# Reading the moving tiles of f32r products by 64-byte pieces, in six different orders

## The chip, the cores and the metric

The kernel runs on one core of a Trainium2 chip. The metric is device time in microseconds for one execution, from the first to the last instruction of the program with what lies around it, as the median of several executions. A profile is one further execution, recorded instruction by instruction. The core has a matrix engine (TensorE, PE in the profile, with its weight loads shown apart as PEld), VectorE (DVE), ScalarE (ACT), GpSimd (POOL), and SyncE (SP), which issues the DMAs.

## The reference

Eight batches of eight heads, 576 tokens, 64 values a head. In each head 32 packed queries p attend over k and v; then the tokens' queries q attend over the 32 packed results, which serve as keys and values. The heads' outputs, side by side, are a row of 512 per token, and all 4608 rows go through a gated feed-forward block with 1536 inner columns.

```python
def sm_attn(qq, kk, vv):
    s = scale * np.matmul(qq, kk.transpose(0, 1, 3, 2))
    s = s - np.max(s, axis=-1, keepdims=True)
    a = np.exp(s)
    a = a / (np.sum(a, axis=-1, keepdims=True) + 1e-09)
    return np.matmul(a, vv)
p_packed = sm_attn(p, k, v)
out = sm_attn(q, p_packed, p_packed)
...
g = x @ w_gate
silu = g * (1.0 / (1.0 + np.exp(-g)))
val = x @ w_val
return (silu * val @ w_out).astype(np.float32)
```

The weights w_gate, w_val and w_out arrive as 64-bit floats, the rest as 32-bit floats.

## The kernel before

A batch's second attention never forms its output. Its weights a2 (one column per token, 32 rows for each head, so two tiles of 128 rows by 576 tokens) are multiplied by a matrix that has the packed values already multiplied into w_gate and w_val. That matrix is built for each batch and each pair of inner chunks by `m_mm` (L586, with `by_head`, L267).

The inner dimension is cut into 12 chunks (`fc`) of 128. `gv_chunk` (L619) makes a chunk of gate and a chunk of value for the first or second part of a batch's tokens: 256 and 320 tokens (`NA`, `NB`); odd batches take the 320 first. The moving operand of these products (L633) is a2, with 256 or 320 columns, one per token; the stationary one is the folded matrix. The result, in PSUM, has the inner columns as rows and the tokens as columns. ScalarE takes the SiLU of the gate (L640), VectorE multiplies by the value (L644), and the product becomes the stationary operand of the second multiplication. There `out_mm` (L650, matmuls at L652) takes 128 tokens at a time, with 512 columns of w_out as the moving operand, and adds up over the 12 chunks in an accumulator `acc`. w_out lies in six tiles, one per pair of chunks; `w_[fc // 2][:, fc % 2]` is one chunk of 512 columns.

Both products are done in f32r, a 32-bit type with a shorter mantissa. Each operand is rounded to it (the high part), and what the rounding left is kept as a second f32r tile (the low part); a product is the sum of high x high, high x low and low x high, three matmuls (`mh`/`ml`, `a2h`/`a2l`, `hh`/`hl`, `wo_h`/`wo_l`). In batch 0 the first ten chunks' output products and the first four chunks' gate and value products are plain f32 instead (L828, L787), and its gate and value products are written apart, in `gv` (L774).

Each batch has 64 tokens that fill no whole row tile; those of two batches are kept in `t4`, and after every odd batch their 128 rows are multiplied by w_out in one go, 36 matmuls without a break between them except for other work put in the middle (`mm4`, the tiles named `aux` at L652).

What sets the order: on TensorE the program order by hand, `PROGRAM` for batch 0 and the tables `FIRST` and `LATER` for the attention steps of later batches, which are put in between the pieces of `gv_chunk` and `outs`. The other engines work beside it and are waited for by semaphores. All this is untouched by the change; it touches the matmuls at L633, L652 and L828 and, on the host, the layout of `q` and `w_out`, before either goes to the chip.

Of the kernel before, what the change touches and what calls it, by code (L numbers as in the profile page):

```python
# [20 lines left out]
B, H, S, D = 8, 8, 576, 64  # L21
NP = 32
DM, DF = 512, 1536
P = 128
NPAR, NHP = 2, 4
NFC = DF // P
# [6 lines left out]
NA, NB = 256, 320  # L33
# [3 lines left out]
F64_HI_MOST = float(np.array(0x47EFFFFF, np.int32).view(np.float32))  # L37
SPLIT = 5
PAD = 120
LOW_WORD = -(2.0**-51) * 15 / 16  # L40

PROGRAM = """

# [89 lines left out]
def tile_pack_attention_swiglu(ctx: ExitStack, tc: tile.TileContext, qT, kT, v, vq, pT, wgv, wout, out):  # L133
# [57 lines left out]
    def f64_convert(dst, st, shape):  # L191
# [5 lines left out]
        yield nc.scalar.activation(dst, hi.bitcast(F32), AF.Abs)  # L197
        yield nc.scalar.activation(lo.bitcast(F32), lo.bitcast(U32), AF.Identity, bias=minus_two, scale=LOW_WORD)
        yield nc.vector.tensor_scalar(dst, dst, F64_HI_LEAST, F64_HI_MOST, op0=ALU.max, op1=ALU.min)
# [3 lines left out]
    sts, wos, wo_h, wo_l = {}, {}, {}, {}  # L203
# [58 lines left out]
    def by_head(outs, lhs, rhs):  # L262

        for hp in range(NHP):
            for par in range(NPAR):
                r = slice(64 * par, 64 * par + 64)
                nc.tensor.matmul(outs[par][32 * hp : 32 * hp + 32], lhs(r, hp), rhs(r, hp), start=True, stop=True)  # L267
# [90 lines left out]
    def s1_scale(b):  # L358
        pp = pool.tile([P, NPAR * D + PAD], F32, tag="pp", bufs=1, name="pp")[:, : NPAR * D].rearrange(
            "p (r d) -> p r d", r=NPAR  # L360
        )
        nc.vector.tensor_tensor(
            pp,
            pps[b][0][:, : NPAR * D].rearrange("p (r d) -> p r d", r=NPAR),
            st1[b][2][:, 2].unsqueeze(2).broadcast_to([P, NPAR, D]),
            op=ALU.mult,
        )
        pps[b].append(pp)
# [241 lines left out]
    def h_split(src, hi, lo, between=lambda: False, tag=""):  # L610
        hh, hl = (pool.tile([P, 256], F32R, tag=t + tag, bufs=2, name=t) if tag else h_tile(t) for t in ("hh", "hl"))
        copy(hi, hh, src)
        last = between()
        low = lo.tensor_tensor(hl, src, hh.bitcast(F32), op=ALU.subtract)  # L614
        if last:
            pin(low)
        return hh, hl

    def gv_chunk(b, fc, is_b, fill, behind, between):  # L619
        odd = b % 2  # L620
        n = NB if is_b else NA
        off = (0 if odd else 256) if is_b else (320 if odd else 0)
        mh, ml = ms[b, fc // 2]
        ah, al = a2[b]
        f = fc % 2
        pgs = []
        for s in range(2):
            pg = ps_gv.tile([P, 512], F32, tag="gv", name="gv")
            pgs.append(pg)
            i = 0  # L630
            for m_, a_ in ((ml, ah), (mh, al), (mh, ah)):
                for g in range(NPAR):
                    nc.tensor.matmul(  # L633
                        pg[:, :n], m_[:, g, f, s * P : (s + 1) * P], a_[:, g, off : off + n],
                        start=(i == 0), stop=(i == 5),
                    )
                    i += 1
            fill()
        sg = pool.tile([P, NB], F32, tag="sg", bufs=1, name="sg")
        nc.scalar.activation(sg[:, :n], pgs[0][:, :n], AF.Silu)  # L640
        behind()
        hf = pool.tile([P, 256], F32, tag="hf", bufs=2, name="hf")
        o, o4 = (64, 0) if is_b and odd else (0, 256)
        nc.vector.tensor_tensor(hf, pgs[1][:, o : o + 256], sg[:, o : o + 256], op=ALU.mult)  # L644
        if is_b:
            r, r4 = slice(64 * odd, 64 * odd + 64), slice(o4, o4 + 64)
            nc.vector.tensor_tensor(t4[b // 2][:, fc, r], pgs[1][:, r4], sg[:, r4], op=ALU.mult)
        return h_split(hf, nc.scalar, nc.vector, between)

    def out_mm(acc, hh, hl, c, fc):  # L650
        for i, (h_, w_) in enumerate(((hl, wo_h), (hh, wo_l), (hh, wo_h))):
            nc.tensor.matmul(  # L652
                acc[:, :],
                h_[:, c : c + P],
                w_[fc // 2][:, fc % 2],
                start=(fc == 0 and i == 0),
                stop=(fc == NFC - 1 and i == 2),
            )
# [60 lines left out]
    with tc.manual_schedule(engines={mybir.EngineType.PE}):  # L719
# [19 lines left out]
        with tc.manual_schedule(  # L739
# [18 lines left out]
            rows, accs = [], []  # L758
# [33 lines left out]
            def half(i):  # L792
                fc, is_b = order[i]
                if fc // 2 < SPLIT:
                    return h0[fc // 2][:, fc % 2, 256 * is_b : 256 * is_b + 256]
                if i not in hs:
                    hs[i] = [pool.tile([P, 256], F32, tag="hf", bufs=2, name="hf")]
                return hs[i][0]
# [23 lines left out]
            def outs(i):  # L822
                fc, is_b = order[i]
                for c in range(2):
                    if fc // 2 >= SPLIT:
                        out_mm(accs[2 * is_b + c], *hs[i][1:], c * P, fc)
                        continue
                    nc.tensor.matmul(  # L828
                        accs[2 * is_b + c], half(i)[:, c * P : c * P + P], wos[fc // 2][:, fc % 2],
                        start=(fc == 0), stop=(fc == NFC - 1),  # L830
                    )

# [23 lines left out]
            def half_of(f, b):  # L856
# [5 lines left out]

            words = {
                "g": gv, "silu": silu, "h": hmul, "hh": h_high, "hl": h_low, "out": outs,
                "z_scores": lambda x: (None if x else s1_tile(0), s1_scores(0, x)), "z_max": lambda x: s1_max(0, x),
                "z_top": lambda x: s1_top(0), "z_exp": lambda x: s1_exp(0, True), "z_turn": lambda x: s1_turn(0, x),
# [26 lines left out]
        def last_outs(rows, accs, out):  # L893
# [5 lines left out]
            return last  # L899

        behind = last_outs(rows, accs, lambda which: outs(2 * NFC - 2 + which))

        steady[0] = True
        def batch(b, behind):
# [6 lines left out]
            def outs(fc, which, fill=lambda: None):  # L911
                src = (hb if which else ha).pop(fc)
                for c in range(2):
                    out_mm(accs[2 * which + c], *src, c * P, fc)
                    fill()

            for fc in range(NFC):
                count = [0]

                def fill():  # L920
                    count[0] += 1
                    if count[0] == 2:
                        run(fc, 2)
                        if fc == NFC - 1 and b + 1 < B:
                            m_part(b + 1, 0, both)
                        elif fc % 2 and fc + 1 < NFC:
                            m_part(b, (fc + 1) // 2, both)
                    if b == 1 and 1 <= fc <= 2 * SPLIT - 4 and count[0] == 7:
                        wout_high(fc + 3)
                        wout_low(fc + 3)  # L930
                    if count[0] != 2:
                        run(fc, count[0])

                ha[fc] = gv_chunk(b, fc, False, fill, lambda: run(fc, "a"), lambda: run(fc, "ha"))
                m_lows()
                if fc:
                    outs(fc - 1, 0, fill)
                else:
                    behind(0)
                hb[fc] = gv_chunk(b, fc, True, fill, lambda: run(fc, "b"), lambda: run(fc, "hb"))  # L940
                if fc:
                    outs(fc - 1, 1, fill)
                else:
                    behind(1)
                    for x, y in zip((rows, accs), accs_of(b)):
                        x.extend(y)
# [11 lines left out]
            def mm4(*ks):  # L958
                for k in ks:
                    for i in range(2):  # L960
                        out_mm(p4[0], *halves[k], i * P, 2 * k + i)
# [59 lines left out]
```

## Time and profile before

| what | value |
|---|---|
| time, median of 3 runs | 735.1 us (735.01 to 736.07) |
| the profiled execution's own time | 734.87 us |
| its span, first to last instruction | 733.1 us |
| TensorE busy | 723.9 us (99%) |
| VectorE busy | 454.2 us (62%) |
| ScalarE busy | 373.7 us (51%) |
| read from HBM, written | 48.69 MB, 9.49 MB |
| share of 16 DMA engines on the main queue | 21.9% |

A busy share of 99% on TensorE doesn't say that it runs at its best, since matmuls overlap and each row holds the time in which the result drains: two matmuls that start 0.23 us apart can each show 0.39 us. To see what a matmul costs in a stream, one takes the distance of two starts. "Idle before" is the time for which an engine did nothing ahead of the instructions of a group, with what ended it. In names such as `acc<-wo_h,hl` the result stands on the left, then the moving and the stationary operand.

### The profile page before, as it was taken

The page shows a single profiled execution, that of the slowest core. Times are in us where ns is not written, and L with a number is a line of the kernel's source. Part 1 is how long each engine was busy: PE and PEld are TensorE (multiplying, and loading weights), DVE is VectorE, ACT ScalarE, POOL GpSimd, SP SyncE. Part 2 cuts the span into 40 slices and gives each one's busy share as a digit, 9 for nine tenths or more (in the row PEclk, how much of TensorE's full clock was granted, in tenths as well). Part 3 has the DMA queues.
Part 4 walks back from the last instruction along what each step waited for, and adds up shares of the span by engine and source line. Part 5 has one row for each costly group of instructions (what it writes and reads, how often), then busy time and mean ns, then how long its engine had stood idle before and what let it go on. Part 6 is the DMA issues. An engine that isn't in the chain of part 4 may idle for free.

```text
span 733.1 us, 15099 instructions
## 1 busy us (share of the span) xinstructions
PE 723.9 (99%) x6242; PEld 590.4 (81%) x6242; DVE 454.2 (62%) x1009; ACT 373.7 (51%) x668; POOL 2.0 (0%) x13
## 2 busy tenths in 40 slices
PE   8899999999999999999999999999999999999997
PEld 4655667888888888888888888888888888888886
DVE  4999779665755557664764646665574655744333
ACT  3779737754635445553563535654453535533331
POOL 0000000000000000000000000000000000000000
PEclk9999999999999999999999999999999999999999
DMA  9697482310112201302112011102001000010001
GB/s 344 269 346 276 140 315 95 111 73 2 65 58 85 74 1 66 126 4 73 66 48 93 21 57 65 43 19 73 1 2 72 4 2 1 1 59 1 1 1 72
DMA packets 20004, 59.15 MB, mean 81 GB/s; under 512 B 5984, under 2 KB 7008, under 8 KB 17376
## 3 DMA queue, kind: packets, MB, share of 16 engines
q1 hardware_dynamic: 19792, 58.12, 21.9%
q8 instruction: 49, 0.80, 0.5%
q14 instruction: 19, 0.16, 0.1%
q10 hardware_dynamic: 144, 0.07, 0.0%
HBM read 48.69 MB, written 9.49 MB: 79 GB/s over the span
## 4 chain that ended last, share of the span: by engine, by line
PE 96%; DVE 1%; issue 0%; DVEq 0%
PE gv L633 36%; PE acc L652 34%; PE aux L267 7%; PE gv L787 6%; PE acc L828 5%; PE aux L652 4%; PE gv_aux L482 1%; PE gv_aux L398 1%; PE gv_aux L267 1%; DVE w L200 0%; PE acc L726 0%; PE aux L343 0%; DVE w L201 0%; PE aux L324 0%; DVE ot L180 0%; PE aux L398 0%
## 5 line engine op out<-in xcount | busy, mean ns | idle before, releaser
L640 ACT ACTIVATE sg<-gv 128x256 f32<-128x256 f32 (+1 forms) x168 | 69.0, 411 | 175.3 <-PE gv L633 161.6
L644 DVE TENSOR_TENSOR hf<-gv,sg 128x256 f32<-128x256 f32 x168 | 71.0, 422 | 129.8 <-PE gv L633 118.5
L633 PE MATMUL gv<-a2h,ml 128*128 128x256 f32 (+1 forms) x672 | 143.5, 295 | 0.0
L633 PE MATMUL gv<-a2l,mh 128*128 128x256 f32 (+1 forms) x672 | 143.4, 295 | 0.0
L633 PE MATMUL gv<-a2h,mh 128*128 128x256 f32 (+1 forms) x672 | 143.4, 295 | 0.0
L652 PE MATMUL acc<-wo_h,hl 128*128 128x512 f32 x344 | 139.8, 406 | 0.0
L652 PE MATMUL acc<-wo_l,hh 128*128 128x512 f32 x344 | 135.5, 394 | 0.0
L652 PE MATMUL acc<-wo_h,hh 128*128 128x512 f32 x344 | 135.5, 394 | 0.0
L633 PEld LDWEIGHTS gv<-a2h,ml 128*128 128x128 f32 x672 | 116.4, 189 | 15.3 <-ACT sg L803 0.4
L178 ACT CAST hh<-hf 128x256 fp32r<-128x256 f32 x168 | 67.7, 403 | 101.9 <-DVE hf L644 101.8
L633 PEld LDWEIGHTS gv<-a2l,mh 128*128 128x128 f32 x672 | 107.8, 189 | 0.0
L633 PEld LDWEIGHTS gv<-a2h,mh 128*128 128x128 f32 x672 | 107.6, 188 | 0.0
L614 DVE TENSOR_TENSOR hl<-hf,hh 128x256 fp32r<-128x256 f32 x168 | 69.8, 416 | 46.4 <-ACT hh L178 46.3
L652 PEld LDWEIGHTS acc<-wo_h,hl 128*128 128x128 f32 x344 | 64.5, 188 | 28.0 <-issue 19.2
L652 PEld LDWEIGHTS acc<-wo_h,hh 128*128 128x128 f32 x344 | 64.6, 188 | 14.6
L652 PEld LDWEIGHTS acc<-wo_l,hh 128*128 128x128 f32 x344 | 64.6, 188 | 8.3 <-issue 0.2
L571 DVE TENSOR_TENSOR ml<-aux,mh 128x512 fp32r<-128x512 f32 x92 | 58.9, 682 | 5.4 <-ACT mh L597 5.4
L267 PE MATMUL aux<-w,ppt 64*32 64x512 f32 (+1 forms) x784 | 52.1, 588 | 0.9 <-DVE w L201 0.9
L597 ACT CAST mh<-aux 128x512 fp32r<-128x512 f32 x92 | 49.4, 590 | 5.6 <-PE aux L267 1.2
L640 ACT ACT_TABLE_LOAD x30 | 38.5, 1283 | 13.6 <-PE gv L633 9.8
L828 PE MATMUL acc<-wo_f,h 128*128 128x512 f32 x80 | 37.8, 602 | 0.0
L828 PEld LDWEIGHTS acc<-wo_f,h 128*128 128x128 f32 x80 | 14.2, 189 | 16.7 <-issue 16.2
(153 smaller groups left out, 754.3 us busy)
## 6 DMA issues: line engine op xcount, KB each, us to landing
st<-in_wgv SPq DMA_DIRECT2D x12, 1024.0 KB, 7.6
k_t<-in_kT SPq DMA_DIRECT2D x16, 576.0 KB, 4.9
q_t<-in_qT SPq DMA_DIRECT2D x16, 576.0 KB, 4.9
out<-ot SPq DMA_DIRECT2D x36, 256.0 KB, 2.1
v_t<-in_vq SPq DMA_DIRECT2D x6, 1280.0 KB, 5.7
st<-in_wout SPq DMA_DIRECT2D x6, 1024.0 KB, 6.8
v_t<-in_v SPq DMA_DIRECT2D x2, 1024.0 KB, 8.7
p_t<-in_pT SPq DMA_DIRECT2D x7, 64.0 KB, 2.4
```

The costliest lines, as they stand in the source:

```text
L178: e.copy(dst, src)
L267: nc.tensor.matmul(outs[par][32 * hp : 32 * hp + 32], lhs(r, hp), rhs(r, hp), start=True, stop=True)
L398: nc.tensor.matmul(pss[par][NP * j : NP * j + NP, i * SQ : (i + 1) * SQ], p_t[r, 2 * g + i, :], k_t[r, j // 2, 2 * g + i, j % 2 * SQ : j % ...
L571: pin(nc.vector.tensor_tensor(*lows.pop(0), op=ALU.subtract))
L597: nc.scalar.copy(m[0][at], src)
L614: low = lo.tensor_tensor(hl, src, hh.bitcast(F32), op=ALU.subtract)
L633: nc.tensor.matmul(pg[:, :n], m_[:, g, f, s * P : (s + 1) * P], a_[:, g, off : off + n], start=(i == 0), stop=(i == 5),)
L640: nc.scalar.activation(sg[:, :n], pgs[0][:, :n], AF.Silu)
L644: nc.vector.tensor_tensor(hf, pgs[1][:, o : o + 256], sg[:, o : o + 256], op=ALU.mult)
L652: nc.tensor.matmul(acc[:, :], h_[:, c : c + P], w_[fc // 2][:, fc % 2], start=(fc == 0 and i == 0), stop=(fc == NFC - 1 and i == 2),)
L787: nc.tensor.matmul(held[i][s][:, :n], m_[:, g, f, s * P : (s + 1) * P], a_[:, g, off : off + n], start=(j == 0), stop=(j == len(todo) - 1),)
L828: nc.tensor.matmul(accs[2 * is_b + c], half(i)[:, c * P : c * P + P], wos[fc // 2][:, fc % 2], start=(fc == 0), stop=(fc == NFC - 1),)
```

## The change

A moving operand that was read from its first column to its last is read in pieces of 16 columns (64 bytes in each partition), and the order of the pieces is one of six. A pair (folds, sign) names an order: the pieces are dealt into `folds` equal runs; the reader takes the first piece of each run, then the second of each, and so on, and with sign -1 it goes through the runs from their last pieces to their first. Within a piece the columns ascend. `UP`, (1, 1), is the order of before and keeps the plain pattern.

- `GV_WALK`, by batch: batches 0, 1 and 7 as before, 2 descending, 3 two runs backward, 4 two runs forward, 5 four runs forward, 6 four runs backward.
- `OUT_WALK`, by pair of w_out's chunks: pair 0 as before, then descending, two runs backward, two runs forward, four runs forward, four runs backward.

The columns of q (hence of a2, which is made from it column by column) and those of w_out are laid out in HBM so that the walk meets them in their natural order: the results land in PSUM as before, in one run, and all that follows is the same. 256 columns make 16 pieces, 320 make 20, 512 make 32.

Nothing moves: each engine issues the same instructions in the same order, with the same waits, and the same DMAs.

```diff
+LINE = 16
+UP, DOWN = (1, 1), (1, -1)
+GV_WALK = (UP, UP, DOWN, (2, -1), (2, 1), (4, 1), (4, -1), UP)
+OUT_WALK = (UP, DOWN, (2, -1), (2, 1), (4, 1), (4, -1))
...
+def walk(n, way):
+    folds, sign = way
+    lines = n // LINE // folds
+    return (0 if sign > 0 else LINE * (lines - 1)), [(sign * LINE, lines), (LINE * lines, folds), (1, LINE)]
+
+
+def places(n, way):
+    start, ((s0, n0), (s1, n1), (s2, n2)) = walk(n, way)
+    i, j, k = np.ogrid[:n0, :n1, :n2]
+    return (start + s0 * i + s1 * j + s2 * k).ravel()
...
-                        pg[:, :n], m_[:, g, f, s * P : (s + 1) * P], a_[:, g, off : off + n],
+                        pg[:, :n], m_[:, g, f, s * P : (s + 1) * P], walked(a_[:, g, off : off + n], GV_WALK[b]),
...
+    def walked(x, way):
+        if way == UP:
+            return x
+        (p0, pn), (step, n) = x.ap
+        start, dims = walk(n, way)
+        return bass.AP(x.tensor, x.offset + start, [(p0, pn), *((k, m) for k, m in dims if m > 1)])
+
     def out_mm(acc, hh, hl, c, fc):
         for i, (h_, w_) in enumerate(((hl, wo_h), (hh, wo_l), (hh, wo_h))):
             nc.tensor.matmul(
                 acc[:, :],
                 h_[:, c : c + P],
-                w_[fc // 2][:, fc % 2],
+                walked(w_[fc // 2][:, fc % 2], OUT_WALK[fc // 2]),
...
                     nc.tensor.matmul(
-                        accs[2 * is_b + c], half(i)[:, c * P : c * P + P], wos[fc // 2][:, fc % 2],
+                        accs[2 * is_b + c], half(i)[:, c * P : c * P + P],
+                        walked(wos[fc // 2][:, fc % 2], OUT_WALK[fc // 2]),
...
-    qT, kT = heads_t(q), heads_t(k)
+    q_laid = np.empty_like(q)
+    for b in range(B):
+        at = 0
+        for n in (NB, NA) if b % 2 else (NA, NB):
+            q_laid[b][:, at + places(n, GV_WALK[b])] = q[b][:, at : at + n]
+            at += n
+    qT, kT = heads_t(q_laid), heads_t(k)
...
-    wo = np.ascontiguousarray(wo).reshape(NFC, P, DM).view(np.int64)
+    wo_laid = np.empty(wo.shape, wo.dtype).reshape(NFC, P, DM)
+    for fc in range(NFC):
+        wo_laid[fc][:, places(DM, OUT_WALK[fc // 2])] = wo[fc * P : (fc + 1) * P]
+    wo = wo_laid.view(np.int64)
```

## The prediction

> **What bounds the kernel now.** I read the head of the page first, then the chain that ended last, then the groups with shapes kept apart, and last the timeline of TensorE in two stretches. The head and the chain:
>
> ```profile
> span 733.1 us, 15099 instructions
> PE 723.9 (99%) x6242; PEld 590.4 (81%) x6242; DVE 454.2 (62%) x1009; ACT 373.7 (51%) x668; POOL 2.0 (0%) x13
> ...
> PEclk9999999999999999999999999999999999999999
> ...
> PE 96%; DVE 1%; issue 0%; DVEq 0%
> PE gv L633 36%; PE acc L652 34%; PE aux L267 7%; PE gv L787 6%; PE acc L828 5%; PE aux L652 4%; PE gv_aux L482 1%; PE gv_aux L398 1%; PE gv_aux L267 1%; DVE w L200 0%; PE acc L726 0%; PE aux L343 0%; DVE w L201 0%; PE aux L324 0%; DVE ot L180 0%; PE aux L398 0%
> ```
>
> TensorE is the chain: 96% of the span by engine, at a granted clock that never leaves the top digit. L633 and L652 are 36 + 34 + 4 = 74% of it, and L828 another 5%: exactly the matmuls whose moving operand the change reads differently. So no engine stands between the change and the end: what one such matmul gains or loses is gained or lost in full. The spacing of the starts is what counts, since a matmul's own row also holds the time in which its result drains. Two stretches of the timeline of TensorE (columns: start in us, duration, engine, line, operation, tiles, shape, count):
>
> ```profile
> 139.38 0.45 PE L633 MATMUL gv<-a2h,ml 128*128 128x320 f32 x2
> ...
> 140.84 0.45 PE L633 MATMUL gv<-a2h,mh 128*128 128x320 f32 x2
> 141.13 0.39 PE L652 MATMUL acc<-wo_h,hl 128*128 128x512 f32 x1
> ...
> 142.52 0.40 PE L633 MATMUL gv<-a2h,ml 128*128 128x256 f32 x2
> ...
> 143.70 0.40 PE L633 MATMUL gv<-a2h,mh 128*128 128x256 f32 x2
> ...
> 209.42 0.39 PE L652 MATMUL aux<-wo_h,hl 128*128 128x512 f32 x1
> ...
> 214.66 0.39 PE L652 MATMUL aux<-wo_h,hh 128*128 128x512 f32 x1
> 214.88 0.45 PE L633 MATMUL gv<-a2h,ml 128*128 128x320 f32 x2
> ```
>
> Ten matmuls of 320 columns start between 139.38 and 140.84, so 146 ns each; ten of 256 between 142.52 and 143.70, 118 ns each; six of 512 between 141.13 and 142.52, 232 ns each. One column more costs (232 - 118) / 256 = 0.44 ns. In the long stretch that begins at 209.42 twenty-four matmuls of 512 columns fit into 5.46 us, 227 ns each, with the same operands.
>
> **The change part by part.** Every engine issues the same instructions in the same order with the same waits, and no DMA changes its size or its shape: the columns of q and of w_out lie in another order in HBM, and the copies, the splits and the softmax work on them column by column as they lie. These parts cost nothing, and no cover is needed for that. What is left is the read pattern of TensorE's moving operand. How many are affected follows from the rows of the groups, shapes kept apart:
>
> ```profile
> L652 PE MATMUL acc<-wo_h,hl 128*128 128x512 f32 x344 | 139.8, 406 | 0.0
> ...
> L633 PE MATMUL gv<-a2h,ml 128*128 128x320 f32 x336 | 76.5, 309 | 0.0
> ...
> L633 PE MATMUL gv<-a2h,mh 128*128 128x256 f32 x336 | 67.1, 281 | 0.0
> ...
> L828 PE MATMUL acc<-wo_f,h 128*128 128x512 f32 x80 | 37.8, 602 | 0.0
> ...
> L652 PE MATMUL aux<-wo_l,hh 128*128 128x512 f32 x48 | 18.7, 390 | 0.0
> ```
>
> Output products: 344 + 48 = 392 in each of the three terms. Those with pair 0 of w_out stay as they are: seven batches x two chunks x four row tiles = 56 in acc and 8 in aux. So 328 a term, 984 in all, are read in 32 pieces, with 31 jumps between them: 30,504 jumps. Gate and value products: 3 terms x 672 = 2016 over batches 1 to 7; batches 2 to 6 are walked, 1440 of them, half with 16 pieces and half with 20: 720 x 15 + 720 x 19 = 24,480 jumps. L828 (batch 0, plain f32): 64 of its 80 rows, 1984 jumps. Together about **57,000 jumps**. With 0.2% of the time, 1.5 us, as about what a measurement of this kernel can tell from no change, the whole question is whether one jump costs more than 1.5 us / 57,000 = **0.026 ns**, a sixteenth of a column.
>
> No row of before shows TensorE reading a moving operand in pieces. The nearest rows are those of the other engines that read SBUF in pieces, or with a step:
>
> ```profile
> L530 ACT ACTIVATE s<-s 128x576 f32<-128x576 f32 x16 | 11.0, 686 | 5.0 <-DVE s L526 4.9
> ...
> L420 ACT ACTIVATE e<-e 128x576 f32<-128x576 f32 x12 | 8.2, 687 | 0.1
> ...
> L178 ACT CAST hh<-hf 128x256 fp32r<-128x256 f32 x168 | 67.7, 403 | 101.9 <-DVE hf L644 101.8
> ...
> L197 ACT ACTIVATE wo_f<-st 128x1024 f32<-128x1024 f32 x6 | 6.9, 1154 | 2.3 <-DMA st<-in_wout 2.3
> ...
> L229 ACT CAST wo_h<-wo_f 128x512 fp32r<-128x512 f32 x12 | 7.4, 613 | 1.5 <-DVE wo_f L201 1.5
> ```
>
> L420 and L530 are the same exponential over 576 elements; L530 reads one run, L420 four runs of 144 words: 687 against 686 ns, so three jumps cost nothing to see. L197 takes every second word, a jump at every element. ScalarE's adjacent reads cost (613 - 403) / 256 = 0.82 ns an element, so 1024 of them would take 613 + 512 x 0.82 = 1033 ns; L197 took 1154, 0.12 ns a jump (its function is another one, so this is an upper end). VectorE shows the same step:
>
> ```profile
> L614 DVE TENSOR_TENSOR hl<-hf,hh 128x256 fp32r<-128x256 f32 x168 | 69.8, 416 | 46.4 <-ACT hh L178 46.3
> ...
> L201 DVE SCALAR_TENSOR_TENSOR wo_f<-st,wo_f 128x1024 int32<-128x1024 int32 x6 | 7.3, 1220 | 0.1
> ...
> L233 DVE TENSOR_TENSOR wo_l<-wo_f,wo_h 128x512 fp32r<-128x512 f32 x12 | 8.2, 683 | 0.4
> ```
>
> Adjacent: 1.04 ns an element ((683 - 416) / 256), so 1024 would take 683 + 534 = 1217 ns; L201, with one operand read every second word, took 1220. Nothing again.
>
> The bounds of a jump are then 0 (L420, L201), 0.12 ns (L197, + 57,000 x 0.12 = 6.8 us) and, since TensorE takes a column in about half the time that ScalarE takes for an element, and a reader that stops for a column at each jump is the plainest way to lose time, 0.44 ns (57,000 x 0.44 = +25 us). Below nothing the bound is the spare time in the spacing of 512-column matmuls, 232 against 227 ns: 3 x (344 - 56) = 864 walked ones in acc x 5 ns = -4.3 us. I take **0 per jump**: L420 is the row nearest in kind, runs of adjacent 4-byte words with jumps between.
>
> [...]
>
> Could the longer pattern cost time per instruction rather than per jump? This row from the timeline bounds it:
>
> ```profile
> 417.61 0.59 PE L482 MATMUL gv_aux<-v_t,a 128*32 128x32 f32 x16
> ```
>
> Sixteen small matmuls, each with its own weights, take 0.59 us, 37 ns apiece with the drain. So an instruction is taken in within 37 ns, beside the 118 ns of the shortest walked matmul; some 80 ns of cover remain. If that cover were gone, each ns would cost 2424 walked f32r matmuls x 1 ns = 2.4 us.
>
> The sum: 734.87 us (the profiled execution: span 733.1 and 1.8 around it) + 0 = 734.9. That execution lies 0.2 us under the median, so the forecast is **735.1 us**.
>
> **The rivals.** *Slower: TensorE's reader loses time at a jump.* Place: L633 in batches 2 to 6 and L652 at pairs 1 to 5. Price: at 0.12 ns a jump 741.9 us, at a column 760. It decides from 0.026 ns a jump. For it: TensorE takes a column in 0.44 ns where ScalarE takes 0.82, so a hiccup that those engines' rows hide may show here; a reader that fetches ahead in ascending order may miss at the backward steps. And every f32r matmul has little slack. Against it: L420 and L201. A milder form, where only backward or folded orders pay, falls between. Chance 0.23, half of it below 745.
>
> *Faster: the order takes off some of the spacing.* The 232 ns of acc against 227 in the long stretch is a loss that some order might avoid: 735.1 - 4.3 = 730.8 us. Against it: the long stretch reads the same wo_h and wo_l by the same ascending order and has the 227, so the loss goes with what was issued just before, not with how the columns are read. [...] Chance 0.06.
>
> *No effect: only the sequence of addresses differs.* That is the forecast, 735.1, with the chance that is left: 0.71.
>
> **How the numbers follow.** The likeliest case is no change, 735.1, give or take the 1 us between runs. The range leaves out the slower half of the slower rival (0.11) and most of the faster one: 733.4 to 745.0; it takes in the 0.12 ns bound. Faster by over 0.2% 0.06, within 0.2% 0.71, slower by over 0.2% 0.23.
>
> **What would show it.** The spare-row products (L652 into aux) run 24 + 12 in a row after each pair of batches, six with each pair of w_out, hence six with each of the six orders, the old one first: if a jump costs nothing, all keep 227 ns; if it costs a column, the first six keep 227 and the others take 227 + 31 x 0.44 = 241. Batches 2 to 6 must keep the 118 and 146 ns of batches 1 and 7. If the starts keep their spacing and the time still moved, the cause is outside TensorE's reading and the argument above is wrong; if only some orders pay, the rule of one price for every jump is wrong.

## The result and the profile after

The changed kernel takes 741.4 us (741.35 to 741.63 in four runs) against 735.1 us: a ratio of 1.0085, 95% interval 1.0068 to 1.0102, so slower by 6.4 us. I had given no change the best chance; the time lies inside the range.

The page of the profiled execution (741.35 us, of which the span is this), head and chain:

```profile
span 739.6 us, 15099 instructions
PE 730.8 (99%) x6242; PEld 593.6 (80%) x6242; DVE 454.6 (61%) x1009; ACT 374.0 (51%) x668; POOL 2.0 (0%) x13
...
PEclk9999999999999999999999999999999999999999
...
PE 96%; DVE 1%; issue 0%; DVEq 0%
PE gv L651 36%; PE acc L677 34%; PE aux L285 7%; PE gv L812 5%; PE acc L853 5%; PE aux L677 5%; PE gv_aux L500 1%; PE gv_aux L416 1%; PE gv_aux L285 1%; DVE w L218 0%; PE acc L751 0%; PE aux L361 0%; DVE w L219 0%; PE aux L342 0%; DVE ot L198 0%; PE aux L416 0%
```

The lines have moved: L633 is now L651, L652 is L677, L828 is L853. TensorE is busy 6.9 us more, VectorE and ScalarE 0.4 and 0.3 us, and the chain is the same. L853, the plain f32 products of which 64 of 80 rows are walked, kept 37.8 us and a mean of 602 ns. The place that tells the orders apart is the long stretch of spare-row products after batch 1, where the six orders follow one another, six matmuls each. Its timeline, with the first start of each order:

```profile
209.67 0.39 PE L677 MATMUL aux<-wo_h,hl 128*128 128x512 f32 x1
...
211.05 0.40 PE L677 MATMUL aux<-wo_h,hl 128*128 128x512 f32 x1
...
212.46 0.40 PE L677 MATMUL aux<-wo_h,hl 128*128 128x512 f32 x1
...
213.86 0.40 PE L677 MATMUL aux<-wo_h,hl 128*128 128x512 f32 x1
...
215.30 0.46 PE L651 MATMUL gv<-a2h,ml 128*128 128x320 f32 x2
...
217.06 0.39 PE L677 MATMUL aux<-wo_h,hl 128*128 128x512 f32 x1
...
218.47 0.39 PE L677 MATMUL aux<-wo_h,hl 128*128 128x512 f32 x1
...
219.89 0.40 PE L651 MATMUL gv<-a2h,ml 128*128 128x256 f32 x2
```

A sixth of each distance is the price of one matmul: contiguous 1.38 / 6 = 230 ns, descending 235, two runs backward 233, two runs forward 240, four runs forward 235, four runs backward 237. The orders differ, although each of the five new ones has 31 jumps. Averaged over all starts of the trace (distances that hold other work left out), before and after:

| order | 512 columns in acc, before | after | 512 in aux, after | batch: 256 columns | 320 columns |
|---|---|---|---|---|---|
| contiguous | 231.5 | 231.0 | 230.8 | 1: 117.8 | 146.2 |
| descending | 231.5 | 233.6 | 233.6 | 2: 118.1 | 147.2 |
| two runs backward | 231.4 | 232.9 | 233.8 | 3: 119.0 | 148.8 |
| two runs forward | 231.6 | 239.9 | 239.6 | 4: 120.1 | 151.5 |
| four runs forward | 231.6 | 234.3 | 233.9 | 5: 118.8 | 147.0 |
| four runs backward | 230.9 | 237.2 | 238.0 | 6: 119.0 | 146.2 |

(ns from start to start; before, the two right columns are 117.9 and 146.1 in every batch, within 0.2, and aux has 226.7 to 230.3.) Going backward is not what costs: the dearest order, two runs forward, steps through both runs in ascending order. Where the time went: acc has 168 matmuls for each pair, 192 for the last: 168 x (-0.5 + 2.1 + 1.5 + 8.3 + 2.7) + 192 x 6.3 ns = 3.6 us; aux, 24 each, 1.0 us; a2's products, 144 of each size in each batch, 2.2 us. That is 6.8 us, against 6.5 in the spans.

### The profile page after: what moved, and what is told of

The parts are those of the page before. It is cut to its first block, busy times and chain, and to the rows that moved or that the text cites. A ratio compares the mean times of both kernels' runs of the same rounds, so it can differ in the third digit from the quotient of the medians.

```text
span 739.6 us, 15099 instructions
## 1 busy us (share of the span) xinstructions
PE 730.8 (99%) x6242; PEld 593.6 (80%) x6242; DVE 454.6 (61%) x1009; ACT 374.0 (51%) x668; POOL 2.0 (0%) x13
## 4 chain that ended last, share of the span: by engine, by line
PE 96%; DVE 1%; issue 0%; DVEq 0%
PE gv L651 36%; PE acc L677 34%; PE aux L285 7%; PE gv L812 5%; PE acc L853 5%; PE aux L677 5%; PE gv_aux L500 1%; PE gv_aux L416 1%; PE gv_aux L285 1%; DVE w L218 0%; PE acc L751 0%; PE aux L361 0%; DVE w L219 0%; PE aux L342 0%; DVE ot L198 0%; PE aux L416 0%
## 5 line engine op out<-in xcount | busy, mean ns | idle before, releaser
L651 PE MATMUL gv<-a2h,ml 128*128 128x256 f32 (+1 forms) x672 | 144.3, 296 | 0.0
L651 PE MATMUL gv<-a2l,mh 128*128 128x256 f32 (+1 forms) x672 | 144.2, 296 | 0.0
L651 PE MATMUL gv<-a2h,mh 128*128 128x256 f32 (+1 forms) x672 | 144.1, 296 | 0.0
L677 PE MATMUL acc<-wo_h,hl 128*128 128x512 f32 x344 | 141.5, 411 | 0.0
L677 PE MATMUL acc<-wo_l,hh 128*128 128x512 f32 x344 | 136.8, 398 | 0.0
L677 PE MATMUL acc<-wo_h,hh 128*128 128x512 f32 x344 | 136.6, 397 | 0.0
L651 PEld LDWEIGHTS gv<-a2h,ml 128*128 128x128 f32 x672 | 116.8, 188 | 16.3 <-ACT sg L828 0.4
L651 PEld LDWEIGHTS gv<-a2h,mh 128*128 128x128 f32 x672 | 108.1, 188 | 0.0
L651 PEld LDWEIGHTS gv<-a2l,mh 128*128 128x128 f32 x672 | 108.0, 188 | 0.0
L677 PEld LDWEIGHTS acc<-wo_h,hl 128*128 128x128 f32 x344 | 64.7, 188 | 28.2 <-issue 19.2
L677 PEld LDWEIGHTS acc<-wo_h,hh 128*128 128x128 f32 x344 | 64.8, 188 | 16.0
L677 PEld LDWEIGHTS acc<-wo_l,hh 128*128 128x128 f32 x344 | 64.8, 188 | 8.5 <-issue 0.2
L853 PE MATMUL acc<-wo_f,h 128*128 128x512 f32 x80 | 37.8, 602 | 0.0
L853 PEld LDWEIGHTS acc<-wo_f,h 128*128 128x128 f32 x80 | 14.2, 189 | 16.7 <-issue 16.2
```

What stands on the lines that cost most here:

```text
L651: nc.tensor.matmul(pg[:, :n], m_[:, g, f, s * P : (s + 1) * P], walked(a_[:, g, off : off + n], GV_WALK[b]), start=(i == 0), stop=(i == 5),)
L677: nc.tensor.matmul(acc[:, :], h_[:, c : c + P], walked(w_[fc // 2][:, fc % 2], OUT_WALK[fc // 2]), start=(fc == 0 and i == 0), stop=(fc == ...
L853: nc.tensor.matmul(accs[2 * is_b + c], half(i)[:, c * P : c * P + P], walked(wos[fc // 2][:, fc % 2], OUT_WALK[fc // 2]), start=(fc == 0), ...
```

## The experiments

The rival prices were now: one price per jump (0.11 ns would make the 6.4 us), a collision of the moving reads with the next matmul's weight load, or a loss of the reader's own that depends on the order. Four of the runs put stretches of equal matmuls behind the kernel before; each of them is one execution, with a granted clock of 1.0, and a price in them is the distance from a stretch's first start to the next stretch's, divided by 40. The contiguous order of 512 columns, with 128 stationary columns that start on a multiple of 256 bytes, took 226.7 to 228.2 ns in its stretches, so a difference of about 1.5 ns between two stretches says nothing.

**Orders, widths and columns.** Added to the kernel before, behind its last instruction: stretches of 40 f32r matmuls into one PSUM tile, here those with 512 columns and 128, 64 or 32 stationary columns.

```diff
+        def read(x, at, *dims):
+            return bass.AP(x.tensor, x.offset + at, [x.ap[0], *dims])
+        mv, wt = wo_l[0][:, 0], wo_h[5]
+        N = 40
+        pt = ps()
+        for i in range(N):
+            nc.tensor.matmul(pt[:128, :512], wt[:, 0, 0:128], read(mv, 0, (16, 16), (256, 2), (1, 16)), start=(i == 0), stop=(i == N - 1))
...
```

> The kernel before, with 20 stretches of 40 f32r matmuls added at its end, each stretch one order of reading, one width of the stationary operand and one number of columns. Two theories. Reader theory: the moving operand's reader alone loses time, by the order: with 512 columns about 227 ns a matmul for ascending, 233 descending, 233 two runs backward, 240 two runs forward, 234 to 237 for four runs, at 128, 64 and 32 stationary columns alike; and the loss grows with the columns: two runs forward 120 ns at 256, 150 at 320, 180 at 384, ascending 113, 142, 170. Collision theory: the next matmul's weight load and the moving reads get in each other's way, and the order decides how often: with 64 stationary columns half of the loss over 213 ns goes (ascending 220, two runs forward 227), with 32 three quarters (217, 220); and the loss per matmul is about the same at 256 as at 512 columns. One price per jump, whatever the order: 234 ns for all five new orders at 512 columns.

The timeline of the stretches (start, length of the 40 together). L992 is contiguous, L995 descending, L998 two runs backward, L1001 two runs forward, L1004 four runs forward; L1019 and L1031 are two runs forward with 64 and 32 stationary columns:

```profile
728.65 9.23 PE L992 MATMUL aux<-wo_l,wo_h 128*128 128x512 f32 x40
737.72 9.50 PE L995 MATMUL aux<-wo_l,wo_h 128*128 128x512 f32 x40
747.05 9.50 PE L998 MATMUL aux<-wo_l,wo_h 128*128 128x512 f32 x40
756.39 9.76 PE L1001 MATMUL aux<-wo_l,wo_h 128*128 128x512 f32 x40
765.99 9.49 PE L1004 MATMUL aux<-wo_l,wo_h 128*128 128x512 f32 x40
775.32 9.70 PE L1007 MATMUL aux<-wo_l,wo_h 128*128 128x512 f32 x40
...
812.60 9.76 PE L1019 MATMUL aux<-wo_l,wo_h 128*64 128x512 f32 x40
822.20 9.36 PE L1022 MATMUL aux<-wo_l,wo_h 128*64 128x512 f32 x40
...
850.06 9.76 PE L1031 MATMUL aux<-wo_l,wo_h 128*32 128x512 f32 x40
859.66 6.03 PE L1034 MATMUL aux<-wo_l,wo_h 128*128 128x320 f32 x40
865.52 6.29 PE L1037 MATMUL aux<-wo_l,wo_h 128*128 128x320 f32 x40
871.65 4.95 PE L1040 MATMUL aux<-wo_l,wo_h 128*128 128x256 f32 x40
876.44 4.96 PE L1043 MATMUL aux<-wo_l,wo_h 128*128 128x256 f32 x40
881.24 7.12 PE L1046 MATMUL aux<-wo_l,wo_h 128*128 128x384 f32 x40
```

Start to next start, by 40: 227, 233, 234, 240, 233 ns, and 238 for four runs backward (L1007, to the next start at 784.85). Two runs forward take 240 ns at 64 columns (812.60 to 822.20) and at 32 (850.06 to 859.66) as well: for this order a weight load a quarter as wide takes nothing off, which speaks against the collision theory as it was put. The reader theory, the same at every width, doesn't hold either: at 64 stationary columns two runs backward and four runs forward (L1022, 822.20 to 831.40) fell from 233 to 230 ns, what the contiguous order takes at that width, and four runs backward from 238 to 235. So the width of the stationary operand has a part in it. In the rows from L1034 on contiguous and two runs forward alternate: 320 columns 147 and 153 ns, 256 columns 120 and 120. The reader theory had 113 for the contiguous 256 and 142 for the 320: missed. At 256, 320, 384 and 512 columns a contiguous f32r matmul of these stretches costs 0.4167 ns a column ((226.7 - 120.0) / 256; over 512 columns 213.3 ns, which is the 213 of the expectation) and **13.3 ns more**, within 0.6 ns; and two runs forward lose nothing at 256 columns.

**Distances and pieces.** The same frame, with two runs 2 to 32 pieces apart, and with other lengths of the pieces. Here and in the later sets only the pattern of the moving operand is printed, one line for a stretch.

```diff
+read(mv, 0, (16, 16), (32, 2), (1, 16))
...
+read(mv, 0, (4, 64), (256, 2), (1, 4))
+read(mv, 0, (64, 4), (256, 2), (1, 64))
...
```

> The kernel before, with 26 stretches of 40 f32r matmuls of 512 columns at its end: two runs read alternately by 64-byte pieces with the runs 2 to 32 pieces apart; two runs 1 KB apart by pieces of 16, 32, 128, 256 and 512 bytes; and the contiguous order, and two runs forward, with the stationary operand starting at other columns. If a jump has one price, all distances give the same time and the loss over 227 ns goes with the number of jumps: 13 ns at 64-byte pieces, 6.5 at 128, 3 at 256, 27 at 32, 53 at 16. If the loss is a clash of consecutive pieces in one part of the memory, the distance decides: some distances stay at 227 and others reach 240 or more, with a period in the distance. If the weight load's place matters (collision theory), the shifted stationary operand changes the time; by the reader theory it doesn't.

All thirteen distances gave 240 ns, so the clash that the expectation had, which would go with the distance, is not what costs. With the runs 1 KB apart, pieces of 16, 32, 64, 128, 256 and 512 bytes gave 250, 243, 240, 237, 227 and 227 ns. The rows for 16, 32, 128, 256 and 512 bytes:

```profile
853.84 10.17 PE L1031 MATMUL aux<-wo_l,wo_h 128*128 128x512 f32 x40
863.84 9.89 PE L1034 MATMUL aux<-wo_l,wo_h 128*128 128x512 f32 x40
873.57 9.63 PE L1037 MATMUL aux<-wo_l,wo_h 128*128 128x512 f32 x40
883.04 9.27 PE L1040 MATMUL aux<-wo_l,wo_h 128*128 128x512 f32 x40
892.14 9.23 PE L1043 MATMUL aux<-wo_l,wo_h 128*128 128x512 f32 x40
901.21 9.49 PE L1046 MATMUL aux<-wo_l,wo_h 128*128 128x512 f32 x40
```

127 jumps cost 23 ns, 63 cost 17, 31 cost 13, 15 cost 10, and 7 nothing beyond the 1.5 ns: no price per jump. L1046 is contiguous reading again, with the stationary operand starting 64 bytes later: 233 ns in place of 227. That agrees with neither theory as I had put it, since the weight load's place does count for the contiguous order; for two runs forward it made no difference (240 at every start tried); the last set has descending at 236 ns with a start 64 bytes later, in place of 233.

**One half of the change alone.** w_out walked and a2 contiguous, then the other way:

```diff
-GV_WALK = (UP, UP, DOWN, (2, -1), (2, 1), (4, 1), (4, -1), UP)
+GV_WALK = (UP,) * 8
```

> The changed kernel with the batches' a2 read contiguously as before; only w_out is read in six orders. From the spacing of starts in the changed kernel's trace (pairs 1 to 5 slower by 2.1, 1.4, 8.3, 2.7 and 6.3 ns in acc, 7 to 13 in aux): about +4.3 us, 739.4. One price per jump (0.11 ns): +3.5 us.

739.6 us, ratio 1.0059 (1.0042 to 1.0075): +4.3 us by the ratio, as the spacing had it (4.6 between the medians); 3.5 lies in the interval too.

```diff
-OUT_WALK = (UP, DOWN, (2, -1), (2, 1), (4, 1), (4, -1))
+OUT_WALK = (UP,) * 6
```

> The changed kernel with w_out read contiguously as before; only batches 2 to 6 read a2 in five orders. From the spacing of starts in the changed kernel's trace: +2.2 us, 737.3, half of it in batch 4 (two runs forward). One price per jump (0.11 ns): +2.7 us, the same in each of the five batches.

736.6 us, ratio 1.0022 (1.0013 to 1.0032): +1.6 us, less than either number, though 2.2 lies in the interval. The distances of the starts say where a part of the rest is: those of 256 and 320 columns rose as in the changed kernel (batch 4: 120.1 and 151.3), while the contiguous matmuls of 512 columns in acc fell from 231.4 to 231.1 on the mean, 0.3 us for the 1032 of them. The two halves add up to most of the whole: 4.3 + 1.6 = 5.9 of the 6.4 us.

**The slowest order everywhere.** One price per jump and a price per order part by 10 us here.

```diff
-GV_WALK = (UP, UP, DOWN, (2, -1), (2, 1), (4, 1), (4, -1), UP)
-OUT_WALK = (UP, DOWN, (2, -1), (2, 1), (4, 1), (4, -1))
+GV_WALK = ((2, 1),) * 8
+OUT_WALK = ((2, 1),) * 6
```

> All walked matmuls of batches 1 to 7, and all of w_out, in the one order that was slowest, two runs forward by 64-byte pieces. If each order has its own cost, as the changed kernel's trace shows for it (239.9 against 231.5 ns in acc, 239.6 against 228 in aux, 120.1 against 117.9 at 256 columns, 151.5 against 146.1 at 320): 1032 x 8.4 + 144 x 12 + 1008 x (2.2 + 5.4) ns = +18.1 us, 753.1. One price per jump (0.11 ns, 71,000 jumps): +7.9 us, 742.9.

752.5 us, ratio 1.0238 (1.0224 to 1.0252), +17.5 us. The price per jump is out by 9.6 us, the price per order by 0.6.

**Longer pieces.** Pieces of 256 bytes: w_out in the same six orders, a2 descending alone.

```diff
-LINE = 16
+LINE = 64
-GV_WALK = (UP, UP, DOWN, (2, -1), (2, 1), (4, 1), (4, -1), UP)
+GV_WALK = (UP, UP) + (DOWN,) * 5 + (UP,)
```

> The changed kernel with pieces of 64 columns (256 bytes) in place of 16: w_out in the same six orders, a2 of batches 2 to 6 descending. If the array leaves the reader about 13 ns a matmul and only what the reader loses beyond it shows, pieces this long cost nothing (two runs at 256 bytes kept 227 ns): 735.1, within 0.2%. If a walked pattern costs by being one, whatever its pieces (2 to 8 ns each): +6 us, 741. One price per jump (0.11 ns, 11,200 jumps): +1.3 us, 736.3.

735.5 us, ratio 1.0004 (0.9995 to 1.0013): nothing. The groups of this kernel against those of the changed one (line, shape, count, busy us, mean ns), first the long pieces:

```profile
L677 PE MATMUL acc<-wo_h,hl 128*128 128x512 f32 x344 | 139.8, 407 | 0.0
...
L651 PE MATMUL gv<-a2h,ml 128*128 128x320 f32 x336 | 76.5, 309 | 0.0
```

then the 64-byte pieces:

```profile
L677 PE MATMUL acc<-wo_h,hl 128*128 128x512 f32 x344 | 141.5, 411 | 0.0
...
L651 PE MATMUL gv<-a2h,ml 128*128 128x320 f32 x336 | 77.0, 310 | 0.0
```

The long pieces have back, to the tenth of a us, what the kernel before shows in the prediction's rows. So neither a pattern of two or three dimensions, nor going backward, nor another layout in HBM costs anything here; the short pieces do.

**Columns, and half the rate.** Thirty more stretches, among them the same orders in plain f32 and on bf16 copies of the tiles.

```diff
+read(mv, 304, (-16, 20), (1, 16))    # 320 columns
+read(mv, 368, (-16, 24), (1, 16))    # 384 columns
+mf, wf = mv.bitcast(F32), wt.bitcast(F32)
...
```

> The kernel before with 30 more stretches of 40 matmuls at its end. Slack theory: a f32r matmul takes the longer of two times, the array's (columns x 0.4167 ns + 13.3) and the reader's (columns x 0.4167 ns + its own loss); the reader loses 0.83 ns for each 64-byte piece with two runs forward, 0.63 descending. So: two runs forward as fast as contiguous at 128 and 192 columns (67, 93 ns) and 210 against 200 at 448; descending as fast as contiguous at 192, 256 and 320, 175 against 173 at 384, 204 against 200 at 448; pieces of 128 bytes free at 256 and 384 columns, pieces of 256 bytes free in every order at 512; plain f32, which takes 429 ns for each of two passes, free in any order. A price per jump that always shows: every walked stretch is slower than the contiguous one by its jumps x 0.2 to 0.43 ns, also at 192 and 256 columns (+2.4 to +6.5 ns).

Descending at 320, 384 and 448 columns (L1022, L1025, L1028); 256 columns in two runs 1 KB apart by pieces of 32, 16 and 128 bytes (L1040, L1043, L1046); plain f32 contiguous and two runs forward (L1073, L1076); bf16 contiguous, two runs forward and descending by 64-byte pieces (L1079, L1082, L1085; of the first, one record is missing). A plain f32 matmul leaves two records, hence x80:

```profile
773.21 6.03 PE L1022 MATMUL aux<-wo_l,wo_h 128*128 128x320 f32 x40
779.08 7.23 PE L1025 MATMUL aux<-wo_l,wo_h 128*128 128x384 f32 x40
786.15 8.34 PE L1028 MATMUL aux<-wo_l,wo_h 128*128 128x448 f32 x40
...
812.28 5.10 PE L1040 MATMUL aux<-wo_l,wo_h 128*128 128x256 f32 x40
817.22 5.36 PE L1043 MATMUL aux<-wo_l,wo_h 128*128 128x256 f32 x40
822.42 4.92 PE L1046 MATMUL aux<-wo_l,wo_h 128*128 128x256 f32 x40
...
898.37 34.49 PE L1073 MATMUL aux<-wo_l,wo_h 128*128 128x512 f32 x80
932.71 34.50 PE L1076 MATMUL aux<-wo_l,wo_h 128*128 128x512 f32 x80
967.04 8.80 PE L1079 MATMUL aux<-mbt,wbt 128*128 128x512 bf16 x39
975.67 8.80 PE L1082 MATMUL aux<-mbt,wbt 128*128 128x512 bf16 x40
984.30 8.80 PE L1085 MATMUL aux<-mbt,wbt 128*128 128x512 bf16 x40
```

Descending: 147 ns at 320 columns, no loss; 177 at 384 (174 contiguous), 204 at 448 (203 contiguous, where I had said 200). Two runs forward: 214 at 448 (210 expected). At 128 and 192 columns the orders tried all take 110 to 112 ns, not 67 and 93: something else, which these stretches don't show, sets that time. Pieces of 128 bytes were free at 256 columns (119 ns) but not at 384 (177 against 174): missed. Pieces of 256 bytes were free in all three orders tried at 512. Pieces of 32 and 16 bytes do lose at 256 columns: 123 and 130 ns against 120. Plain f32 takes 429 ns a record in both orders, and bf16 takes 216 ns in all three. Plain f32 reads the same 32 pieces, but takes 429 ns over 512 columns where f32r takes 227. bf16 asks for half as many bytes in the same time as f32r (2 for each 0.42 ns); it has half as many pieces too, and a stationary operand of half the bytes, so its stretches don't say which of these makes the orders free.

**What the short pieces lose.** A last set asked whether 256-byte blocks that are left early, steps back, or patterns as such are to blame.

```diff
+read(mv, 48, (64, 8), (-16, 4), (1, 16))    # blocks ascending, descending inside
+read(mv, 464, (-64, 8), (1, 64))            # blocks descending, 64 bytes off
+read(mv, 0, (64, 8), (0, 4), (1, 16))       # one piece of a block, four times
+read(mv, 0, (32, 32), (1, 16))              # ascending, every second piece
+read(mv, 0, (128, 8), (1, 64))              # ascending, every second 256 bytes
...
```

> The kernel before with 23 more stretches of 40 f32r matmuls of 512 columns at its end. What makes the reader lose time? Block theory: it fetches aligned blocks of 256 bytes and loses when a stretch of reading leaves a block before it is used up. Then a pattern of pieces that visits the addresses in ascending order is free (227 ns), and so are all orders that finish a block before they leave it, also descending inside it (by 64 or by 128 bytes) or reading one piece of it four times; orders that take 64 bytes of each block and come back lose (233 to 240). Direction theory: a step back loses, whatever the block: descending inside ascending blocks 233, ascending inside descending blocks 227. Pattern theory: a pattern of short runs costs as such: 64-byte pieces in ascending order 233 to 240 as well. Pieces of 256 bytes that start 64 bytes off a multiple of 256 cost about as much as the contiguous order 64 bytes off (229).

The rows of four of them, descending inside ascending blocks, one piece four times, and ascending over every second 64-byte and every second 256-byte piece:

```profile
738.43 9.50 PE L995 MATMUL aux<-wo_l,wo_h 128*128 128x512 f32 x40
...
784.39 9.85 PE L1010 MATMUL aux<-wo_l,wo_h 128*128 128x512 f32 x40
...
878.51 9.76 PE L1040 MATMUL aux<-wo_l,wo_h 128*128 128x512 f32 x40
...
897.20 9.23 PE L1046 MATMUL aux<-wo_l,wo_h 128*128 128x512 f32 x40
```

With the next starts at 747.77, 794.08, 888.11 and 906.26 that is 233, 242, 240 and 227 ns. So the block theory falls (no block was left early in the first two), and the direction theory too (the third never steps back). The patterns whose pieces join up in ascending order had been merged into a contiguous read when they were compiled (the program has one run of 512 for them, and they took 227 to 228 ns), so they don't test the pattern theory; every second 64-byte piece, which can't be merged, took the 240 ns that it expected. What the stretches of 512 columns with 128 stationary ones agree on is the length of the run: contiguous runs of 256 bytes or more that start on a multiple of 256 from the tile's start took 227 to 228 ns in every order tried, and shorter ones 231 to 250. Runs of 256 bytes that start 64 bytes off took 229 ns, like contiguous reading from there.

## Why the prediction was wrong

- **That TensorE bounds, and that a loss of such a matmul shows in full**: right. The spacings add up to 6.8 us, the span grew by 6.5.
- **That nothing else moves**: right. With 256-byte pieces the same walk and the same layout cost nothing.
- **The price of a jump, 0**: this is the step that failed. The 57,000 jumps were put at nothing and cost 6.4 us. I took the row nearest in kind, ScalarE's four runs, as evidence for TensorE. It could show nothing: its runs were 576 bytes long, above the 256 bytes from which TensorE too took 227 ns, and ScalarE read 4 bytes in 0.82 ns where f32r reads 4 in 0.42. Plain f32 products, which take 0.84 ns a column (429 / 512), read the same 64-byte runs for nothing on TensorE as well. In place of the 0 stands a loss that depends on the length of the run, the order and the columns: 1.5 to 8.3 ns for each walked matmul of 512 columns in acc, and up to 5.4 ns for one of a2's products.
- **The slower rival**: its sign came out, its mechanism, one price for every jump, did not; that its number (741.9 at ScalarE's 0.12 ns a jump) came close to 741.4 is luck. 31 jumps cost 1.5 to 8 ns in acc and 7 to 13 in a steady stream, by their order, and the slowest order everywhere took 9.6 us more than a price per jump gives.
- **The cover per instruction** (80 ns): right, as the long pieces show (ratio 1.0004).
- **The spacing of 232 against 227 as a gain**: no order brought the acc matmuls to 227, though with walked a2 products the contiguous ones fell to 230 or 231. Why acc takes 231 where a long stretch takes 227 stays open.

What replaces it, as far as it was shown: short runs of an f32r moving operand cost time on TensorE, as the two halves (+4.3 and +1.6 us) and the long pieces (ratio 1.0004) show. How they cost it is argued. In the stretches a contiguous f32r matmul takes 0.4167 ns a column and 13.3 ns besides, but for 448 columns, where it took 203.2 and not 200.0; in the kernel's own stream it takes 117.9 at 256 columns. I read this as two times of which the longer counts: reading in short runs takes longer per column, but the 13.3 ns hide the first part, which is why 256 columns hardly suffer and 512 most: two runs forward lose 0, 7, 6, 11 and 13 ns at 256, 320, 384, 448 and 512. The hiding is argued from this dependence and from the descending order, free to 320 columns in the stretches, and not shown otherwise; nothing in the profile shows the reading by itself.

The shortest pieces speak against the simple form of it, a loss for every piece of which the first 13.3 ns are hidden. At 256 columns pieces of 32 and 16 bytes show 123.4 and 130.0 ns, so the reader's own loss over 256 x 0.4167 = 106.7 ns would be 16.7 and 23.3; twice that over 213.3 ns gives 247 and 260 at 512 columns, where 243 and 250 were measured. From 256 to 512 columns pieces of 16, 32 and 64 bytes all add 120 ns, contiguous reading 107. Still open, then: by what rule the loss grows, why equal runs cost 7 ns in one order and 13 in another, what part the stationary operand has, whose width and start change the pace of some orders and not of two runs forward, and what the unit of 256 bytes is.

## What to carry to other kernels

A row of another engine, with longer runs and at half the rate, doesn't price a read of TensorE: ScalarE's four runs showed 1 ns (687 against 686), TensorE's 32 pieces cost 7 to 13 ns in the stretches. Let f32r moving operands be read in contiguous runs of at least 256 bytes that start on a multiple of 256 bytes from the start of the tile (227 to 228 ns for 512 columns, where shorter runs took 231 to 250), and likewise start the stationary operand there (233 ns with a start 64 bytes later); the order of such runs was free wherever it was tried, so a layout may choose it. Measure a cost at two sizes before it is given a price per piece: two runs forward lost nothing at 256 columns and 13 ns at 512.

## What else the runs showed

The start of the stationary operand counts too: with contiguous reading of 512 columns 227 ns at starts 0, 256, 512, 768 and 1024 bytes, 233 at 64 and at 128. A moving operand that starts 64 or 128 bytes off took 229 and 233. A narrower stationary operand made the contiguous stream slower, not faster: 227 ns at 128 columns, 230 at 64, 231 at 32. The row for 64, and the next start, from the timeline of the first set of stretches:

```profile
784.85 9.37 PE L1010 MATMUL aux<-wo_l,wo_h 128*64 128x512 f32 x40
794.06 9.50 PE L1013 MATMUL aux<-wo_l,wo_h 128*64 128x512 f32 x40
```
